# A decode step on one core: the score matmuls of a K chunk as a four-pass loop on TensorE

## The chip, the cores and the metric

The kernel runs on one core of one Trainium2 chip. The metric is device time in microseconds (us) for one execution, lower is better. Times are medians of several executions. A profile is one execution recorded by the hardware profiler; its span goes from the first to the last instruction on the core.

The engines named here are TensorE (PE; its weight loads are PEld), VectorE (DVE), ScalarE (ACT), GpSimd (POOL) and SyncE (SP). Each runs its own list of instructions in order and waits on semaphores that others raise. In this kernel SyncE issues the large transfers.

## The reference

One token passes through a transformer block: layer norm, grouped-query attention against a long cache, layer norm, a gated feed-forward layer, with residual sums. `x` is 1 x 1024; there are 32 query heads and 4 K/V heads of 128, the cache holds 65536 positions, the feed-forward layer is 3584 wide, everything in bf16.

```
q = (layernorm(x) @ wq) as 32 heads of 128
scores = q . k * 128**-0.5          # each K/V head serves 8 query heads
o = softmax(scores) . v             # over 65536 positions
h = x + o @ wo
h2 = h + (gelu(layernorm(h) @ w_gate) * (layernorm(h) @ w_up)) @ w_down
```

K and V together are 134 MB, the weights 39 MB: each byte is read once.

## The kernel before

**Layout.** A K/V head has 65536 positions, 512 on each of 128 partitions. A chunk is 64 of these 512, that is 128 x 64 positions of 128 numbers, 2 MB; a head has NCH = 8 chunks of K and 8 of V. One load brings two chunks of K (4 MB), or two or four chunks of V (4 or 8 MB), into `ring`, a buffer of NSL = 4 slots of 4 MB that every large transfer uses in turn (`load`, L238, and `chunk`, L76). A slot can be loaded again when whatever read it has finished.

**Scores of a chunk** (`k_chunk`, L251). VectorE takes the chunk in NS = 4 quarters (s) and transposes each in blocks of 32 x 32, as 4-byte pairs (L264), from the ring into a tile `kt`. So it is VectorE that frees a K slot, after eight such transposes (two chunks). For each quarter TensorE runs four matmuls (jt = 0 to 3, L268), whose weights are parts of `qs`, a copy of the head's queries spread with zeros (`make_qs`, GpSimd, L222 and L226). All 16 add into one PSUM bank `qk`. Afterwards (`score_chunk`, L272) VectorE transposes `qk` into `sc` (L278) and takes a maximum (L279). `sc` holds four chunks, so a head has two of them.

**Softmax of a head** (`softmax_head`, L281). Over the eight maxima VectorE and TensorE form one bias per query head (L284 to L294: maximum, transpose, maximum, diagonal, broadcast, scaling); then ScalarE computes 16 exponentials (L301) from the two `sc` tiles into two `pt` tiles, with row sums.

**V of a head** (`v_chunk`, L308). TensorE multiplies `pt` with V straight from the ring, 16 matmuls per chunk (L317), and so frees V slots. After the last chunk ScalarE copies the sum (L326), TensorE folds it in eight matmuls (L329), VectorE copies the outcome to `o_raw` (L331).

**Order.** The loop at L335 goes over the four heads g and their chunks ci: K chunk, then the scores of the chunk before, at the head's end the last scores and the softmax, and after chunks 3 and 7 four V chunks of the head before. The V of the last head comes after that, then the output projection and the feed-forward layer, whose weights go through the same ring. The code does not write out waits. The framework that builds the program records which tiles each instruction reads and writes, orders the instructions of each engine by priority and by its own estimate of when they are ready, and sets the semaphores. Within an engine the order is then fixed. What comes out for VectorE in a K load is: eight transposes L264, then L278, L279, L278, L279.

```
for g in range(Hkv):
    for ci in range(NCH):
        k_chunk(g, ci)
        if ci >= 1:
            score_chunk(g, ci - 1)
        if ci == NCH - 1:
            score_chunk(g, ci)
            softmax_head(g)
```

SyncE's order of loads is: two of wq, four of K of head 0, two of K of head 1, V of head 0 (4 MB and 4 MB), two of K of head 1, V of head 0 (8 MB), and from there on two loads of K and 8 MB of V in turn, with the last 16 MB of V, wo, w_gate, w_up and w_down behind them.

## Time and profile before

| what | value |
|---|---|
| median of 3 executions | 410.69 us (410.64 to 410.88) |
| profiled execution, span | 408.8 us |
| outside the span (median less span) | 1.9 us |
| moved by transfers | 173 MB, mean 424 GB/s |
| TensorE busy | 228.8 us, 56% |
| VectorE busy | 205.1 us, 50% |
| ScalarE busy | 36.6 us, 9% |
| GpSimd busy | 43.5 us, 11% |
| mean granted TensorE clock | 0.787 of full speed |

The profiled execution's own time is not listed beside the others; its span is the one in the table. In a timeline line the numbers are the start and the length in us, then engine, source line, operation, output and input, with the shape, and xN for N instructions merged; in brackets stand the idle time before it and what ended it. In a line of waits the numbers are the total in us, how many, and the longest. In a group's line they are, behind the bar, the busy time in us, the mean of one in ns, and the engine's idle time before them with what ended it. A matmul's duration includes its tail, which overlaps the next one: the rate is better read from the distance of weight loads, one of which goes with each matmul.

### The profile page before, as it was taken

To read this page: it belongs to the slowest core of one execution; us is meant where nothing else is said; L and a number is where in the kernel's file an instruction comes from. 1 tells how busy PE (TensorE), PEld (TensorE's weight loads), DVE (VectorE), ACT (ScalarE), POOL (GpSimd) and SP (SyncE) were. 2 spreads that over 40 slices of the span, in tenths; PEclk is the share of its full clock that TensorE was granted. 3 is DMA by queue.
4 is the path that set the end of the run, shared out by engine and by line. 5 is a ranking of instruction groups with operands and counts; after the bars stand their busy time and mean duration, and the time that the engine had idled before them with its cause. 6 is when DMAs were issued, how large, how long until landed. Compare 5 with 4: busy or idle time off the path is not lost.

```text
span 408.8 us, 3981 instructions
## 1 busy us (share of the span) xinstructions
PE 228.8 (56%) x1623; PEld 99.0 (24%) x1623; DVE 205.1 (50%) x263; ACT 36.6 (9%) x136; POOL 43.5 (11%) x150
## 2 busy tenths in 40 slices
PE   1337677688388367844765575576351425275045
PEld 1112222133133132311222222222120113143024
DVE  2118999999299239905980696089500001012010
ACT  1000000070000520000008000000340000000000
POOL 8123000300000400000002400000400100002000
PEclk9966989988888668868996689669885656566688
DMA  8999999999999999999999999999999999999995
GB/s 359 410 462 406 442 430 418 449 415 452 417 457 430 402 444 458 423 410 428 472 417 420 418 478 394 428 462 430 436 418 449 430 442 425 427 432 423 416 410 212
DMA packets 5144, 173.26 MB, mean 424 GB/s; under 512 B 643, under 2 KB 647, under 8 KB 1031
## 3 DMA queue, kind: packets, MB, share of 16 engines
q1 hardware_dynamic: 5079, 173.02, 98.4%
q8 instruction: 12, 0.20, 0.2%
q14 instruction: 5, 0.04, 0.0%
q10 hardware_dynamic: 48, 0.00, 0.0%
HBM read 173.02 MB, written 0.00 MB: 423 GB/s over the span
## 4 chain that ended last, share of the span: by engine, by line
DMA 68%; DVE 22%; PE 5%; issue 4%; SPq 0%; ACT 0%
DMA ring<-in_A_k_cache_dram 42%; DVE kt L264 19%; DMA ring<-in_A_wo_dram 8%; DMA ring<-in_B_w_up_dram 7%; DMA ring<-in_A_v_cache_dram 7%; DMA ring<-in_B_w_down_dram 4%; PE qk_ps L268 2%; PE at_ps L410 2%; PE acc_ps L317 1%; DVE sc L278 1%; DVE mx L279 1%; SPq L100 0%; PE mxT_ps L286 0%; PE d_ps L489 0%; DVE gm L288 0%
## 5 line engine op out<-in xcount | busy, mean ns | idle before, releaser
L268 PE MATMUL qk_ps<-kt,qs 128*128 128x512 bf16 x512 | 141.0, 426 | 59.8 <-DVE kt L264 46.2
L264 DVE STREAM_TRANSPOSE kt<-ring 128x1024 f32<-128x1024 f32 x128 | 146.2, 1208 | 45.4 <-DMA ring<-in_A_k_cache_dram 45.4
L268 PEld LDWEIGHTS <-qs 128*128 128x128 bf16 x512 | 53.7, 105 | 143.8 <-issue 95.1
L317 PE MATMUL acc_ps<-ring,pt 128*32 128x512 bf16 x512 | 44.7, 526 | 50.6 <-DMA ring<-in_A_v_cache_dram 50.6
L301 ACT ACTIVATE pt<-sc,nbias 128x256 bf16<-128x256 f32 x64 | 31.5, 494 | 261.9 <-DVE nbias L294 261.9
L317 PEld LDWEIGHTS <-pt 128*32 128x32 bf16 x512 | 18.4, 127 | 75.2 <-issue 51.8
L331 DVE COPY o_raw<-o_ps 128x8 f32<-128x8 f32 x4 | 0.7, 167 | 48.1 <-PE o_ps L329 48.1
L278 DVE STREAM_TRANSPOSE sc<-qk_ps 128x512 f32<-128x512 f32 x32 | 22.1, 692 | 1.0 <-PE qk_ps L268 1.0
L279 DVE TENSOR_REDUCE mx<-sc 128x8 f32<-128x512 f32 x32 | 22.0, 688 | 1.1
L222 POOL MEMSET qs<- 128x2048 bf16 x4 | 7.2, 1802 | 94.8 <-PE qk_ps L268 94.8
L186 PEld LDWEIGHTS <-xz 128*32 128x32 bf16 x192 | 6.8, 124 | 33.0 <-issue 16.1
L226 POOL COPY qs<-qsel 32x32 bf16<-32x32 bf16 x64 | 11.2, 247 | 16.6 <-DVE qsel L217 15.9
L324 DVE TENSOR_TENSOR lsum<-lpart 128x8 f32<-128x8 f32 x4 | 0.7, 164 | 24.2 <-ACT pt L301 24.2
L186 PE MATMUL qw_ps<-ring,xz 128*32 128x512 bf16 x64 | 7.2, 625 | 9.4 <-DMA ring<-in_A_wq_dram 9.4
L410 PE MATMUL at_ps<-ring,o2z 128*32 128x512 bf16 x64 | 6.6, 594 | 10.4 <-DMA ring<-in_A_wo_dram 10.4
L301 ACT ACTIVATION_READ_ACCUMULATOR pt<-sc,nbias 128x1 f32 x64 | 12.0, 187 | 0.0
L186 PE MATMUL u_ps_w<-ring,xz 128*32 128x512 bf16 (+1 forms) x64 | 4.5, 450 | 10.7 <-DMA ring<-in_B_w_up_dram 10.7
L427 DVE TENSOR_TENSOR h_col<-hc_ps,x_col 128x8 f32<-128x8 f32 x1 | 0.2, 166 | 19.5 <-PE hc_ps L420 19.5
L199 DVE STREAM_TRANSPOSE u_ps_r<-u_ps_w 128x512 f32<-128x512 f32 (+1 forms) x2 | 1.2, 629 | 14.1 <-PE u_ps_w L186 14.1
L199 DVE STREAM_TRANSPOSE q_r<-qw_ps 128x512 f32<-128x512 f32 x2 | 1.3, 696 | 13.6 <-PE qw_ps L186 13.6
L489 PE MATMUL d_ps<-ring,actz 128*32 128x128 bf16 x108 | 5.0, 263 | 5.6 <-DMA ring<-in_B_w_down_dram 5.5
L380 POOL MEMSET cz<- 128x256 bf16 x1 | 0.3, 311 | 72.6 <-PE qk_ps L268 72.6
(104 smaller groups left out, 92.0 us busy)
## 6 DMA issues: line engine op xcount, KB each, us to landing
ring<-in_A_k_cache_dram SPq DMA_DIRECT2D x16, 4096.0 KB
ring<-in_A_wq_dram SPq DMA_DIRECT2D x2, 4096.0 KB
ring<-in_A_v_cache_dram SPq DMA_DIRECT2D x2, 4096.0 KB
ring<-in_B_w_gate_dram SPq DMA_DIRECT2D x1, 7168.0 KB
ring<-in_B_w_up_dram SPq DMA_DIRECT2D x1, 7168.0 KB
ring<-in_B_w_down_dram SPq DMA_DIRECT2D x1, 4096.0 KB
ring<-in_B_w_down_dram SPq DMA_DIRECT2D x1, 1792.0 KB
ring<-in_B_w_down_dram SPq DMA_DIRECT2D x1, 768.0 KB
```

Of the source, the lines that this page charges most:

```text
L186: nc.tensor.matmul(banks[t // 4][32 * q:32 * q + 32, :], lhsT=rows_z[:, ci, :], rhs=w, start=first, stop=last, tile_position=(0, 32 * q))
L199: nc.vector.transpose(out=r[:, o:o + n].rearrange("p (e j) -> p e j", j=32) if sizes else r[:, o:o + n], in_=src)
L222: nc.gpsimd.memset(qs[:], 0.0)
L226: nc.gpsimd.tensor_copy(out=qs[rows, :, s, SQ * i + s:SQ * (i + 1):NS], in_=qsel[rows, :, g * rep:(g + 1) * rep])
L264: nc.vector.transpose(out=kt[:], in_=k32[:, s * W:(s + 1) * W])
L268: nc.tensor.matmul(qk[:], lhsT=st["qs"][:, jt, s, :], rhs=mv[:, :, J, :, t], start=(s == 0 and jt == 0), stop=(s == NS - 1 and jt == 3))
L278: nc.vector.transpose(out=sc.rearrange("p n h s -> p (n h s)"), in_=qk[:])
L279: nc.vector.tensor_reduce(out=st["mx"][:, :, ci], in_=sc.rearrange("p n h s -> p h n s"), axis=AX.XY, op=ALU.max)
L301: nc.scalar.activation(out=pt[:].rearrange("p c n h s -> p (c n) h s")[:, :, r, :], in_=sc[:].rearrange("p c n h s -> p (c n) h s")[:, :, ...
L317: nc.tensor.matmul(acc[32 * c:32 * c + 32, :], lhsT=pt[:, ci % CPH, n, :, :].rearrange("p h s -> p (h s)"), rhs=v_sb[:, n:CH:NN, :], start ...
L410: nc.tensor.matmul(at_ps[32 * q:32 * q + 32, :], lhsT=o2z[:, c, :], rhs=wv[:, c, :].rearrange("k (p s c) -> k s p c", s=DS, c=C4)[:, s], s ...
L489: nc.tensor.matmul((d_ps, d_odd)[q // 2][32 * q:32 * q + 32, :], lhsT=a_row[:, AZ - m:AZ - m + 32], rhs=w_row[:, j * OB:(j + 1) * OB], sta ...
```

## The change

The four quarters of a chunk are transposed into one `kt` tile of the whole chunk. Then VectorE sets the PSUM bank to zero, and TensorE runs its 16 matmuls as a loop of four passes (one per quarter) with four matmuls in each; the addresses in `qs` and `kt` come from a register. The loop stands in a critical section: the framework treats it as one unit, which TensorE enters when what was ordered before it is there, and the program is cut into blocks around it, so that each engine gets a jump at each cut. Since the loop's body is the same in every pass, the matmuls always add to what the bank holds. `kt` has 2 buffers of a chunk instead of 6 of a quarter, `sc` has 2 instead of 3. The scores of a chunk follow one chunk later also across heads, so the last scores and the softmax of a head come after the first K chunk of the next one.

```diff
-    ktpool = ctx.enter_context(tc.tile_pool(name="ktpool", bufs=6))
+    ktpool = ctx.enter_context(tc.tile_pool(name="ktpool", bufs=2))
...
-    scpool = ctx.enter_context(tc.tile_pool(name="scpool", bufs=3))
+    scpool = ctx.enter_context(tc.tile_pool(name="scpool", bufs=2))
...
         qk = ps_qk.tile([P, NN * SQ], F32, name="qk_ps", tag="qk")
+        kt = ktpool.tile([P, NS * W], F32, name="kt", tag="kt")
         for s in range(NS):
-            kt = ktpool.tile([P, W], F32, name="kt", tag="kt")
-            nc.vector.transpose(out=kt[:], in_=k32[:, s * W:(s + 1) * W])
-            mv = kt[:].bitcast(BF16).rearrange("p (n j b t) -> p n j b t", n=NN, j=2, t=2)
-            for jt in range(4):
-                J, t = divmod(jt, 2)
-                nc.tensor.matmul(qk[:], lhsT=st["qs"][:, jt, s, :], rhs=mv[:, :, J, :, t],
-                                 start=(s == 0 and jt == 0), stop=(s == NS - 1 and jt == 3))
+            nc.vector.transpose(out=kt[:, s * W:(s + 1) * W], in_=k32[:, s * W:(s + 1) * W])
+        mv = kt[:].bitcast(BF16).rearrange("p (s n j b t) -> p s n j b t", s=NS, n=NN, j=2, t=2)
+        nc.vector.memset(qk[:], 0.0)
+        with tc.tile_critical(no_gpsimd_drain=True):
+            with nc.tensor.Fori(0, NS) as i:
+                for jt in range(4):
+                    J, t = divmod(jt, 2)
+                    nc.tensor.matmul(qk[:], lhsT=st["qs"][:, jt, bass.ds(i, 1), :].rearrange("p s m -> p (s m)"),
+                                     rhs=mv[:, bass.ds(i, 1), :, J, :, t].rearrange("p s n b -> p (s n) b"),
+                                     start=False, stop=False, skip_group_check=True)
         st[("qk", ci)] = qk
...
+    def score_step(g, ci):
+        score_chunk(g, ci)
+        if ci == NCH - 1:
+            softmax_head(g)
+
+    late = None
     for g in range(Hkv):
         for ci in range(NCH):
             k_chunk(g, ci)
-            if ci >= 1:
-                score_chunk(g, ci - 1)
-            if ci == NCH - 1:
-                score_chunk(g, ci)
-                softmax_head(g)
+            if late:
+                score_step(*late)
+            late = g, ci
             if g >= 1 and ci % VB == VB - 1:
                 for vi in range(ci - VB + 1, ci + 1):
                     v_chunk(g - 1, vi)
+    score_step(*late)
```

## The prediction

> **What bounds the kernel now.** I read the page's totals first, then the DMA queue's own waits, then the timeline of each engine in the first head, then the groups by form.

> ```profile
> span 408.8 us, 3981 instructions
> PE 228.8 (56%) x1623; PEld 99.0 (24%) x1623; DVE 205.1 (50%) x263; ACT 36.6 (9%) x136; POOL 43.5 (11%) x150
> DMA  8999999999999999999999999999999999999995
> q1 hardware_dynamic: 5079, 173.02, 98.4%
> ```

> The transfers bound it: 173 MB, the queue 98.4% busy in every slice, engines half idle. A 4 MB load takes 9.7 us (K data reach VectorE at 150.16, 188.95, 228.12 and 266.90, four loads apart: 38.8/4). So the change costs nothing until it makes a load start late. A load starts when its ring slot is free, and K slots are freed by VectorE:

> ```profile
> SPq L247 <- DVE kt L264: 158.3, 15, 12.5
> SPq L247 <- PE acc_ps L317: 33.0, 6, 6.4
> ```

> How early a load is issued is the margin. In the first head VectorE sets the pace, with TensorE close behind it:

> ```profile
> 33.97 0.14 PEld L268 LDWEIGHTS <-qs 128*128 128x128 bf16 x1 [0.28 <-issue]
> 34.39 0.14 PEld L268 LDWEIGHTS <-qs 128*128 128x128 bf16 x1 [0.28 <-issue]
> 36.89 4.25 PEld L268 LDWEIGHTS <-qs 128*128 128x128 bf16 x20 [0.22 <-issue]
> 55.69 9.12 DVE L264 STREAM_TRANSPOSE kt<-ring 128x1024 f32<-128x1024 f32 x8
> 64.73 0.68 DVE L278 STREAM_TRANSPOSE sc<-qk_ps 128x512 f32<-128x512 f32 x1
> ...
> 67.39 9.12 DVE L264 STREAM_TRANSPOSE kt<-ring 128x1024 f32<-128x1024 f32 x8
> 89.39 12.10 SPq L247 DMA_DIRECT2D ring<-in_A_k_cache_dram  x2
> 102.31 3.64 PE L317 MATMUL acc_ps<-ring,pt 128*32 128x512 bf16 x64
> ```

> A pair of chunks (one load) takes VectorE 67.39-55.69 = 11.7 us: eight transposes 9.12, two score transposes, two maxima. The eighth K load is issued near 101.2 (89.39+12.10, less the 0.33 that an issue takes); the transfer ahead of it lands at 111.41 (where VectorE next waits for K data). The margin is 10 us over the five periods since the first pair: above 11.7+2.0 = 13.7 us per pair the transfers run dry.

> ```profile
> L264 DVE STREAM_TRANSPOSE kt<-ring 128x1024 f32<-128x1024 f32 x128 | 146.2, 1208 | 45.4 <-DMA ring<-in_A_k_cache_dram 45.4
> L278 DVE STREAM_TRANSPOSE sc<-qk_ps 128x512 f32<-128x512 f32 x32 | 22.1, 692 | 1.0 <-PE qk_ps L268 1.0
> L279 DVE TENSOR_REDUCE mx<-sc 128x8 f32<-128x512 f32 x32 | 22.0, 688 | 1.1
> L469 DVE MEMSET d_ps<- 128x128 f32 x1 | 0.2, 165 | 0.1
> L424 DVE MEMSET hc_ps<- 128x8 f32 x1 | 0.1, 65 | 0.0
> L301 ACT ACTIVATE pt<-sc,nbias 128x256 bf16<-128x256 f32 x64 | 31.5, 494 | 261.9 <-DVE nbias L294 261.9
> ```

> **The change, part by part.** In the changed program VectorE's order per pair is: eight K transposes, score transpose of each chunk, two maxima, two memsets. TensorE enters each loop behind a list of waits: all four transposes of its chunk and, because a critical section closes everything ordered before it, whatever stands earlier in the program: for the pair's first loop (A) also the first transpose of the second chunk, for its second (B) the score transpose of the first chunk; besides, loads already issued and exponentials already ordered. So A starts after five transposes, B after A and a score transpose, and VectorE's second score transpose waits for the end of B, with the next pair's transposes queued behind it. Before, matmuls ran four per transpose, beside them; now B runs beside nothing. The period is a sum:

> - Five transposes, 9.12/8 each: 5.70. The other three hide under loop A.
> - Loop A, 16 matmuls. TensorE has idled some 9 us (3.0+5.7) and starts slow: in the fence above weight loads come 427 ns apart after an idle stretch, ten of them, then 20 in 4.25 us, 212 ns. 10x0.4275+6x0.2125 = 5.55.
> - Loop control shows in no row. A pass: below, nothing, as the sequencer may run ahead of the array; above, a weight load plus one sequencer step as long as a DMA issue (0.10+0.33 = 0.43). I take one exposed weight load, 0.105 (L268, PEld), four per loop: 0.42, since a weight load is what a branch most directly delays. Entry: below 0.14 (a transpose ends at 33.44, the first matmul starts at 33.58), above 0.7 (SyncE's wait at the start barrier); taken 0.45. Exit: below 0.17 (the tail of a matmul, 378 against 212 ns apart), above 1.0; taken 0.55, since drain and two semaphore hops come in series. A: 6.97.
> - Score transpose 0.70, between A and B.
> - Loop B, at 0.2125 without a pause: 3.40+0.42+1.00 = 4.82.
> - Score transpose 0.70, two maxima 2x0.67, two new memsets. 65 ns at 8 columns, 165 at 128: 0.83 ns per column, 0.49 at 512. Sum 3.02.

> Period 21.2 us against 11.7, bounds 19.0 (no control cost beyond 0.17 exit and 0.14 entry) and 25.2 (upper ones). It passes 13.7, so the chain of pairs sets the time in head 0, and also later: a head moves eight loads, 77.6 us, 19.4 per pair.

> [...]

> Moved work. Softmax of a head now follows the next head's first transposes. In head 0 to 1, VectorE's order mixes these with scores, so they cover a loop: an estimated 4 us saved. In the other two boundaries VectorE stands in order behind the copy of the previous head's output, so TensorE's V block (3.64), its copy and fold (0.7+1.06+0.3), then maximum, diagonal and bias (1.8, from 290.55 to 292.35) come before the next transposes: 7.5 less the 3.0 that VectorE does meanwhile. The next loop also waits for 16 exponentials, 7.9 us against 5.7 of transposes. 4.4+2.2, twice: 13. The middle V block of a head hides beside scores and transposes. SyncE's queue keeps its order; its loads wait for slots. The V blocks stand behind the loops on TensorE and free V slots with them, later by the same periods. Waits on issued loads bind once: the first loop A needs the second K load, 9.9 after the first, against 5.7: 4.1. Later loads land over 4 us ahead of the loop that names them. Fewer buffers: kt holds two chunks where it held one and a half, so VectorE still runs a pair ahead at most; a third sc buffer is missed only when a head's first scores come before the first eight exponentials, 3.9 us, which the five transposes cover. Branches on the other engines lie in their idle time.

> Sum: first transpose 32.3, +4.1, fifteen periods 318.0, -4, +13, last eight transposes 9.1: K is done at 372.5. Then the V load that waits for it starts, 2.0 later (the last output transfer, 406.81 to the end), with an empty queue. Before, that V load could start at 295.9, when its predecessor landed (TensorE's V block waits until 295.97); from there the span had 112.9 us of transfers at full rate, which are unchanged. 372.5+2.0+112.9 = 487.4. Outside the span lie 410.7-408.8 = 1.9 us, the median less the span: **489 us**, 19% slower.

> **The rivals.**
> 1. Cheaper loops: period 19.0, 33 us less, 456. For: the sequencer may hide all control under slow matmuls. Against: below 19.4 the transfers bind in the later heads and keep part of it.
> 2. Dearer loops: a pass at 0.43 adds 8x0.33 = 2.6 per pair, 39 us: 528. For: each pass reads registers and branches; against: ten matmuls run slow and cover it.
> 3. TensorE stays slow through both loops (pauses at each pass keep it so): +1.29 and +3.44 per pair, 71 us: 560. Against: four matmuls per 1.14 us transpose, a quarter of it idle, stayed fast in the pair at 44 us.
> [...]
> 5. Not slower: transfers hide it all, 410.7. It needs a period under 13.7, hence A+B under 4.3 us; 32 matmuls at 212 ns are 6.8. Only if loops run beside the transposes, VectorE's own 12.9 setting the pace, would it hold; the listed waits speak against it.

> **How the numbers follow.** Forecast 0.55, rivals 0.12, 0.14, 0.09, 0.07, 0.03. 489 is the forecast's. The range leaves out 560 and 410.7 and the thin ends: 452 to 540. About 0.2% can be told from no change here. Faster 0.01, same 0.02, slower 0.97.

> **What to look for.** Pair starts of K transposes 21 us apart in every head, and not 38.8 per two; VectorE's second score transpose waiting about 5 us for TensorE; loop matmuls 427 then 212 ns apart; DMA share near 84%, with gaps in slices from the first head to the third; a full queue only after the last K transpose near 372. Wrong if matmuls of a chunk start before its fourth transpose, if loop B is far from 4.8 us, or if SyncE's K issues still come 10 us ahead of need.

## The result and the profile after

The changed kernel takes 493.12 us (median of 4 executions, 491.98 to 493.64) against 410.74 us: 1.2005 times as long, with an interval of 1.199 to 1.2019. The forecast was 489.0 with a range of 452 to 540. The profiled execution took 493.34 us, with a span of 491.6 and a mean granted clock of 0.785 (0.787 before), so the clock is not what moved.

The totals of the page after the change:

```profile
span 491.6 us, 5288 instructions
PE 232.5 (47%) x1623; PEld 99.4 (20%) x1623; DVE 218.1 (44%) x295; ACT 36.6 (7%) x136; POOL 43.6 (9%) x150
DMA  8999995727087999999589989958956999999994
q1 hardware_dynamic: 5079, 173.02, 83.5%
```

Read the rows beside those of before. No engine does much more work: TensorE 232.5 us against 228.8, VectorE 218.1 against 205.1 (32 memsets more). The same 173.02 MB pass through the queue, but it is 83.5% busy instead of 98.4%, and the row of slices, counted from 0, shows where: gaps from slice 6 to slice 30 (74 to 381 us), then a full queue nearly to the end. One slice (123 to 135 us) is empty. While K is read, the queue now runs dry again and again, though several slices between the gaps are still full: the transfers no longer set the pace there.

Who holds SyncE's loads back, from the waits of the DMA queue:

```profile
SPq L247 <- DVE kt L264: 271.9, 15, 29.4
SPq L247 <- PE acc_ps L321: 74.2, 6, 13.1
```

Before, the 15 K loads waited 158.3 us for VectorE to free a slot, now 271.9, and the longest wait has grown from 12.5 to 29.4 us. The V loads wait 74.2 instead of 33.0. So VectorE reads K late. Why it does stands in the groups and the waits:

```profile
L271 PE MATMUL qk_ps<-kt,qs 128*128 x512 | 156.8, 453 | 171.1 <-DVE kt L264 93.1
L264 DVE STREAM_TRANSPOSE kt<-ring 128x1024 f32<-128x1024 f32 x128 | 146.4, 1205 | 3.7 <-DMA ring<-in_A_k_cache_dram 3.7
L282 DVE STREAM_TRANSPOSE sc<-qk_ps 128x512 f32<-128x512 f32 x32 | 22.9, 716 | 136.5 <-PEq L267 136.4
L283 DVE TENSOR_REDUCE mx<-sc 128x8 f32<-128x512 f32 x32 | 19.9, 657 | 0.0
L266 DVE MEMSET qk_ps<- 128x512 f32 x32 | 15.5, 485 | 3.0 <-issue 0.2
```

The K transposes waited 45.4 us for data before and wait 3.7 now: data are always there. VectorE's idle time has moved to the score transpose, 136.4 us, released by TensorE's sequencer at L267, the critical section. TensorE in turn waits 93.1 us for the K transposes. Each waits for the other, once per pair of chunks.

One such pair in the timeline (the second of head 0; weight loads left out except in the pause that they show):

```profile
58.68 9.09 DVE L264 STREAM_TRANSPOSE kt<-ring 128x1024 f32<-128x1024 f32 x8
65.17 5.34 PE L271 MATMUL qk_ps<-kt,qs 128*128 x16 [9.58 <-DVE kt L264]
...
70.68 0.72 DVE L282 STREAM_TRANSPOSE sc<-qk_ps 128x512 f32<-128x512 f32 x1 [2.91 <-PEq L267]
...
72.15 4.39 PE L271 MATMUL qk_ps<-kt,qs 128*128 x16 [1.65 <-DVE sc L282]
73.29 0.58 PEld L271 LDWEIGHTS qk_ps<-kt,qs 128*128 x4 [0.50 <-issue]
...
76.72 0.72 DVE L282 STREAM_TRANSPOSE sc<-qk_ps 128x512 f32<-128x512 f32 x1 [5.33 <-PEq L267]
77.36 1.24 DVE L283 TENSOR_REDUCE mx<-sc 128x8 f32<-128x512 f32 x2
78.70 1.03 DVE L266 MEMSET qk_ps<- 128x512 f32 x2
79.64 3.46 DVE L264 STREAM_TRANSPOSE kt<-ring 128x1024 f32<-128x1024 f32 x3
```

From 58.68 to 79.64 is one period, 20.96 us, against 11.7 before. Loop A starts after the fifth transpose (which ends at 64.4), loop B after the first score transpose, and VectorE idles 5.33 us under loop B with the next pair's transposes behind it.

### The profile page after: what moved, and what is told of

The parts are those of the page before. It is cut to its first block, busy times and chain, and to the rows that moved or that the text cites. A ratio compares the mean times of both kernels' runs of the same rounds, so it can differ in the third digit from the quotient of the medians.

```text
span 491.6 us, 5288 instructions
## 1 busy us (share of the span) xinstructions
PE 232.5 (47%) x1623; PEld 99.4 (20%) x1623; DVE 218.1 (44%) x295; ACT 36.6 (7%) x136; POOL 43.6 (9%) x150
## 3 DMA queue, kind: packets, MB, share of 16 engines
q1 hardware_dynamic: 5079, 173.02, 83.5%
HBM read 173.02 MB, written 0.00 MB: 352 GB/s over the span
## 5 line engine op out<-in xcount | busy, mean ns | idle before, releaser
L271 PE MATMUL qk_ps<-kt,qs 128*128 x512 | 156.8, 453 | 171.1 <-DVE kt L264 93.1
L264 DVE STREAM_TRANSPOSE kt<-ring 128x1024 f32<-128x1024 f32 x128 | 146.4, 1205 | 3.7 <-DMA ring<-in_A_k_cache_dram 3.7
L271 PEld LDWEIGHTS qk_ps<-kt,qs 128*128 x512 | 56.5, 110 | 269.9 <-issue 245.8
L282 DVE STREAM_TRANSPOSE sc<-qk_ps 128x512 f32<-128x512 f32 x32 | 22.9, 716 | 136.5 <-PEq L267 136.4
L321 PE MATMUL acc_ps<-ring,pt 128*32 128x512 bf16 x512 | 32.3, 410 | 22.3 <-DMA ring<-in_A_v_cache_dram 14.4
L305 ACT ACTIVATE pt<-sc,nbias 128x256 bf16<-128x256 f32 x64 | 31.5, 494 | 140.6 <-DVE nbias L298 140.6
L321 PEld LDWEIGHTS <-pt 128*32 128x32 bf16 x512 | 15.5, 103 | 38.6 <-issue 29.2
L330 ACT COPY acc_sb<-acc_ps 128x512 f32<-128x512 f32 x4 | 2.3, 586 | 245.2 <-PE acc_ps L321 245.2
L283 DVE TENSOR_REDUCE mx<-sc 128x8 f32<-128x512 f32 x32 | 19.9, 657 | 0.0
L266 DVE MEMSET qk_ps<- 128x512 f32 x32 | 15.5, 485 | 3.0 <-issue 0.2
L226 POOL COPY qs<-qsel 32x32 bf16<-32x32 bf16 x64 | 11.2, 247 | 17.2 <-DVE qsel L217 16.5
L186 PE MATMUL g_ps_w<-ring,xz 128*32 128x512 bf16 (+1 forms) x64 | 5.2, 505 | 6.6 <-DMA ring<-in_B_w_gate_dram 6.6
```

The costliest lines, as they stand in the source:

```text
L186: nc.tensor.matmul(banks[t // 4][32 * q:32 * q + 32, :], lhsT=rows_z[:, ci, :], rhs=w, start=first, stop=last, tile_position=(0, 32 * q))
L226: nc.gpsimd.tensor_copy(out=qs[rows, :, s, SQ * i + s:SQ * (i + 1):NS], in_=qsel[rows, :, g * rep:(g + 1) * rep])
L264: nc.vector.transpose(out=kt[:, s * W:(s + 1) * W], in_=k32[:, s * W:(s + 1) * W])
L266: nc.vector.memset(qk[:], 0.0)
L271: nc.tensor.matmul(qk[:], lhsT=st["qs"][:, jt, bass.ds(i, 1), :].rearrange("p s m -> p (s m)"), rhs=mv[:, bass.ds(i, 1), :, J, :, t].rearr ...
L282: nc.vector.transpose(out=sc.rearrange("p n h s -> p (n h s)"), in_=qk[:])
```

## The experiments

The changes that the new kernel makes together were taken apart. Each kernel was timed against the kernel before on the same chip (410.60 to 410.72 us there).

**e1: the late order alone**, in the kernel before.

```diff
+    late = None
     for g in range(Hkv):
         for ci in range(NCH):
             k_chunk(g, ci)
-            if ci >= 1:
-                score_chunk(g, ci - 1)
-            if ci == NCH - 1:
-                score_chunk(g, ci)
-                softmax_head(g)
+            if late:
+                score_step(*late)
+            late = g, ci
...
+    score_step(*late)
```

> The kernel before with the late order alone: scores and softmax follow one chunk later across heads, matmuls unrolled as before, buffers as before. Theory (the wait chain of the critical loop costs the time): the pair of chunks keeps its 11.7 us on VectorE, so 410.7 us, within 0.5. Rival (the late scores and softmax cost it, through V blocks and exponentials that come later): each of three head boundaries adds 2 to 6 us as in the changed kernel, 415 to 425 us.

Measured: 410.70 us, ratio 1.0 (0.999 to 1.0009). The order of scores and softmax cost nothing by itself here.

**e2: the memset and the always-adding matmuls alone**, in the kernel before.

```diff
+        nc.vector.memset(qk[:], 0.0)
...
-                                 start=(s == 0 and jt == 0), stop=(s == NS - 1 and jt == 3))
+                                 start=False, stop=False, skip_group_check=True)
```

> The kernel before with the memset of the PSUM bank alone, and matmuls that always add. Theory: the pair takes VectorE 11.7 + 2 x 0.485 = 12.7 us, below the 13.7 at which the transfers run dry, so 410.7 us, within 0.5. Rival (VectorE's added work is on the path): 32 x 0.485 = 15.5 us more, 426 us.

Measured: 411.12 us, ratio 1.0014 (1.0005 to 1.0023), 0.4 us.

**e3: all of the change but the loop and its critical section.** The 16 matmuls are written out, one `kt` tile per chunk, two buffers, memset, two `sc` buffers, late order.

```diff
-        with tc.tile_critical(no_gpsimd_drain=True):
-            with nc.tensor.Fori(0, NS) as i:
-                for jt in range(4):
...
+        for s in range(NS):
+            for jt in range(4):
+                J, t = divmod(jt, 2)
+                nc.tensor.matmul(qk[:], lhsT=st["qs"][:, jt, s, :], rhs=mv[:, s, :, J, :, t],
+                                 start=False, stop=False, skip_group_check=True)
```

> The changed kernel with the loop and its critical section taken out: 16 matmuls written out with fixed addresses, one kt tile of a chunk with 2 buffers, memset, 2 sc buffers, late scores. Theory: matmuls start again after the first transpose or at the latest beside the next chunk's; VectorE sets the pace with 12.7 us per pair, 410.7 us, within 1. Rival (the one kt tile with 2 buffers and fewer sc buffers make the chain): a period near 19 to 21 us stays and with it more than 450 us.

Measured: 410.70 us, ratio 1.0003 (0.9993 to 1.0012). So the whole loss sits in the loop and the section around it; buffers, tile size, memset and order carry none of it that can be told at this noise.

**e4: the critical section kept, the loop written out inside it.**

```diff
         with tc.tile_critical(no_gpsimd_drain=True):
-            with nc.tensor.Fori(0, NS) as i:
+            for s in range(NS):
                 for jt in range(4):
```

> The changed kernel with the critical section kept, but its 16 matmuls written out instead of the loop of four passes: no registers, no branch per pass. Theory (the unit with its waits is the cost, the passes a small part): the pauses between passes of the second loop go, three of 0.28 us, and some 0.3 to 0.5 us of control; the period falls from 21.0 to about 19.6 us, 15 x 1.4 = 20 us less, 465 to 480 us. Rival (register addresses and branches are the cost): back to 411 us.

Measured: 480.67 us, ratio 1.1708 (1.1686 to 1.173), just above the theory's 480. The timeline of its second pair:

```profile
56.20 9.10 DVE L264 STREAM_TRANSPOSE kt<-ring 128x1024 f32<-128x1024 f32 x8
62.37 5.59 PE L271 MATMUL qk_ps<-kt,qs 128*128 128x512 bf16 x16 [9.26 <-DVE kt L264]
...
68.22 0.72 DVE L281 STREAM_TRANSPOSE sc<-qk_ps 128x512 f32<-128x512 f32 x1 [2.92 <-PEq L267]
69.37 3.66 PE L271 MATMUL qk_ps<-kt,qs 128*128 128x512 bf16 x16 [1.41 <-DVE sc L281]
73.20 0.72 DVE L281 STREAM_TRANSPOSE sc<-qk_ps 128x512 f32<-128x512 f32 x1 [4.26 <-PEq L267]
...
76.12 3.46 DVE L264 STREAM_TRANSPOSE kt<-ring 128x1024 f32<-128x1024 f32 x3
```

The shape of the changed kernel without any loop: a period of 19.9 us. What the loop adds can be read line by line. B takes 3.66 us here and 4.39 there; the first matmul of B follows the score transpose after 0.43 us here (68.94 to 69.37) and 0.75 there (71.40 to 72.15). Of the 82.4 us lost, 12.5 go with the loop and 69.9 remain with the section and its waits. The theory had put some 20 us on the loop, 1.4 per pair, and jumps and entries do save that much here; but loop A took longer without the loop, 5.85 us on average over the 16 pairs against 5.41. It started at other places of the grid on which the granted clock changed (last section): in pairs two to four the slow rate lasted 4.1 to 5.0 us here and 2.9 to 3.4 there.

**e6: two passes of eight matmuls** in place of four of four.

```diff
-            with nc.tensor.Fori(0, NS) as i:
-                for jt in range(4):
+            with nc.tensor.Fori(0, NS // 2) as i:
+                for h in range(2):
+                    for jt in range(4):
...
```

> The changed kernel with two passes of eight matmuls instead of four of four. Theory: the pause between passes shows only where matmuls run fast (0.28 us in the second loop of a pair, hidden under 427 ns matmuls in the first); two pauses fewer in the second loop and up to one in the first, 0.6 to 0.8 us per pair, 9 to 12 us less: 481 to 484 us. Rival (passes are the main cost): half of the 82 us goes, 452 us.

Measured: 486.96 us, ratio 1.1869 (1.1835 to 1.1902). That is 3 us above the theory's 481 to 484; the rival's 452 was far off. The 6.2 us gained are half of the loop's 12.5, but this does not price a pass: the one jump that is left hardly shows (loop B takes 3.7 to 3.8 us in most pairs, against 3.66 written out and 4.3 to 4.4 with four passes). What the loop still costs beside e4 lies mainly in its entry, which stays at 0.75 to 1.05 us where e4 has 0.43 to 0.66.

**e5: the score transposes moved off the chain.** Scores follow two chunks late, and on VectorE each score transpose is ordered behind the K transposes of the chunk two later, so that loops can run beside transposes.

```diff
...
-        nc.vector.transpose(out=sc.rearrange("p n h s -> p (n h s)"), in_=qk[:])
+        tr = nc.vector.transpose(out=sc.rearrange("p n h s -> p (n h s)"), in_=qk[:])
+        tc.add_manual_dep(tr.ins, last_t[0].ins.name,
+                          mybir.DependencyInfo(mybir.DependencyClass.NoSync, mybir.DependencyReason.DATA), reason="order")
...
-            if late:
-                score_step(*late)
-            late = g, ci
+            late.append((g, ci))
+            if len(late) > 2:
+                score_step(*late.pop(0))
...
```

> The changed kernel with loop and critical section, but scores two chunks late, and each score transpose put in VectorE's order behind the transposes of the chunk two later, so that it finds its loop done. Theory in its simplest form (VectorE's wait for the loop just started, with the next transposes queued behind it, is the whole cost): the period falls to VectorE's own 12.9 us or TensorE's two loops with entries, 12 to 13.5 us, and the time to 411 to 425 us. Rival (the critical section's other waits, for loads issued earlier in the order, hold the loops as soon as the chain is shorter): VectorE's transposes wait on kt buffers held by loops that wait for loads, and the time stays at 450 to 475 us.

Measured: 475.17 us, ratio 1.1572 (1.1552 to 1.1591). The simple theory fell. Behind the first pair of head 0 the pairs do come 12.1 to 13.7 us apart (transposes at 49.35, 63.06, 76.22, 88.32), about as it said. So the jumps at the section's block cuts, which every engine still makes here, can't cost much by themselves: they fit into 12.1 to 13.7 us beside everything else. In head 1 the timeline shows something else:

```profile
131.20 0.33 SPq L247 DMA_DIRECT2D ring<-in_A_v_cache_dram  x1
...
133.19 31.69 SPq L247 DMA_DIRECT2D ring<-in_A_k_cache_dram  x2
...
153.86 5.28 PE L273 MATMUL qk_ps<-kt,qs 128*128 x16 [16.65 <-DMA ring<-in_A_v_cache_dram]
159.31 1.25 DVE L266 STREAM_TRANSPOSE kt<-ring 128x1024 f32<-128x1024 f32 x1 [16.70 <-PEq L269]
```

A score loop, which reads no V, waits 16.65 us for an 8 MB load of V, because that load stands before the section in the program. VectorE's transposes queue up behind it for 16.70 us, the K slot stays occupied, and of the two K loads in the third line the second is issued only at 164.5 us (133.19 + 31.69, less the 0.33 of an issue). The load that the loop waits for was issued at 131.20, 1.7 us before the loop ahead of it started; while it moves only one more is issued, and from 154 to 165 us the queue is 66% busy. The second theory, that the section's other waits take over, holds; its range of 450 to 475 was passed by 0.2 us.

**e9: the same order, the loop written out in the section.** Is it the loop's length or the section's list of waits that keeps e5 slow?

```diff
         with tc.tile_critical(no_gpsimd_drain=True):
-            with nc.tensor.Fori(0, NS) as i:
+            for s in range(NS):
                 for jt in range(4):
```

> e5's order (scores two chunks late, score transposes behind later K transposes on VectorE) with the critical section kept but its 16 matmuls written out, no loop. Theory (from head 1 on the waits on issued loads in the critical section bind, whatever the loop costs): 466 to 476 us, at most 9 below e5's 475.2. Rival (the loop's control and entry made e5's matmuls too slow to hide): 411 to 445 us.

Measured: 470.89 us, ratio 1.1451 (1.1423 to 1.148), inside the theory's bounds. The same stall stands at the same place of its timeline:

```profile
151.54 6.40 PE L273 MATMUL qk_ps<-kt,qs 128*128 128x512 bf16 x16 [17.90 <-DMA ring<-in_A_v_cache_dram]
158.11 1.25 DVE L266 STREAM_TRANSPOSE kt<-ring 128x1024 f32<-128x1024 f32 x1 [19.08 <-PEq L269]
```

It is not the only one: by the list of TensorE's waits in this run, score matmuls wait five times for a load of V, 70.8 us in all, the longest 17.9. So the section keeps the kernel slow in either of two ways: through the chain of score transposes when VectorE's order is as the framework writes it, and through waits on loads that it does not read when the chain is shortened. A register-addressed loop outside such a section was not tried.

**e8: no section, but whole chunks.** Does the mere fact hurt that a loop starts with the fourth transpose of its chunk, not with the first? In e3 the quarters were taken in an order that makes the first matmul need the last quarter.

```diff
-        for s in range(NS):
+        for s in (3, 0, 1, 2):
             for jt in range(4):
```

> The written-out matmuls of e3 (no loop, no critical section), but with the chunk's fourth quarter first, so that the first of the 16 matmuls needs the chunk's fourth transpose, as the loop does. Theory (the critical section's list of waits is what costs, not the loss of quarter-by-quarter work by itself): the fourth transpose ends 4.6 us into the pair, 16 slow matmuls' worth of about 5.6 follow, then the second chunk's 3.4, and the second score transpose, two maxima and two memsets end near 15 us: a period of 14 to 15.5 in head 0, against a threshold of 13.7, hidden again later: 411 to 418 us. Rival (starting only when the whole chunk is transposed is most of the loss): periods near 20, 460 or more.

Measured: 410.71 us, ratio 1.0007 (0.9994 to 1.002): no change, where the theory had 411 to 418. Its second and third pairs:

```profile
44.98 4.59 DVE L264 STREAM_TRANSPOSE kt<-ring 128x1024 f32<-128x1024 f32 x4
49.50 0.68 DVE L280 STREAM_TRANSPOSE sc<-qk_ps 128x512 f32<-128x512 f32 x1
...
49.63 10.04 PE L270 MATMUL qk_ps<-kt,qs 128*128 128x512 bf16 x32 [3.13 <-DVE kt L264]
...
56.23 0.72 DVE L280 STREAM_TRANSPOSE sc<-qk_ps 128x512 f32<-128x512 f32 x1 [0.95 <-PE qk_ps L270]
...
58.57 4.59 DVE L264 STREAM_TRANSPOSE kt<-ring 128x1024 f32<-128x1024 f32 x4
```

Without a section the framework may put a chunk's score transpose behind the next four K transposes, and TensorE runs 32 matmuls in one block with VectorE beside it. The pairs come 13.6 and then 12.5 us apart, below or at the prediction's bound of 13.7. Waiting for the whole chunk cost nothing here.

**e7: TensorE kept busy ahead of loop A.** Ten extra matmuls, whose output is not read, run during the first transposes of each pair.

```diff
+        if ci % 2 == 0:
+            warm = misc([P, NN * SQ], F32, "warm")
+            for _ in range(10):
+                nc.tensor.matmul(warm[:], lhsT=st["qs"][:, 0, 0, :], rhs=mv[:, 0, :, 0, :, 0], start=True, stop=True)
```

> The changed kernel with ten extra matmuls, whose output nobody reads, on TensorE during the transposes of the first chunk of each pair, so that its first loop starts fast. Theory: the first loop then takes what the second does, 4.36 instead of 5.1 to 5.3 us, as pauses between passes come into view; 0.8 to 0.9 us per pair, 12 to 14 us less: 479 to 481 us. Rival (the slow start costs its full 10 x 0.215 = 2.1 us per pair): 32 us less, 461 us. If the extra matmuls only delay the loop: no change or slower.

Measured: 469.63 us, ratio 1.1426 (1.1399 to 1.1453): 23.5 us below the changed kernel, between theory and rival, which were both 9 us or more off. Loop A takes 4.31 us in the second pair instead of 5.34. But it runs that fast (4.3 to 4.4 us) in only 8 of the 16 pairs and takes 5.1 to 6.6 in the others, and this is not where most of the gain lies. By the starts of the pairs, the first four pairs together gain 2.3 us (the fifth starts at 118.07 instead of 120.36). The two pairs of the first head boundary gain 4.5 (35.81 instead of 40.32), the three around the second 6.5 (176.21 to 238.70 instead of 181.93 to 250.94), the three around the third 9.1 (259.64 to 320.46 instead of 273.10 to 343.03): 20.1 of the 21.8 us by which the last pair is ahead. The extra matmuls also changed what VectorE does at the boundaries. How much of these gains is the clock and how much the order stays open.

## Why the prediction was right, point by point

**The bound: right; the threshold: only bracketed.** The transfers hide a longer period up to a point: e8's first four periods, 12.8 us on average with one of 13.6, stay hidden, the changed kernel's 21 does not. No run that kept its pairs between 13 and 19 us through a whole kernel was made, so the 13.7 itself was not tested. The queue ran empty where it was predicted, between head 0 and the last K transpose, at 83.5% ("near 84%").

**The period: right in the sum, with errors that cancel.** The eight undisturbed pairs average 21.09 us (20.06 to 22.16), forecast 21.2. So near a hit is luck: in the pair shown loop A with entry and exit took 0.66 us less than forecast, loop B 0.50 more. By terms:

| term | forecast, us | measured, us |
|---|---|---|
| five transposes | 5.70 | 5.7 |
| A: entry | 0.45 | 0.8 |
| A: matmuls and passes | 5.97 | 5.34, its tail included |
| A: exit | 0.55, tail included | 0.17 |
| score transpose | 0.70 | 0.72 |
| B: entry, matmuls and passes, exit | 4.82 | 5.32 (0.75 + 4.39 + 0.18) |
| score transpose, maxima, memsets | 3.02 | 2.92 |

The mis-sized terms are the loop's control. The forecast spread it evenly (0.42 for the passes of each loop). It is not even: in the loop A shown the slow matmuls cover the passes completely (0.427 us apart across them), in loop B each of the three jumps shows: the matmuls on its two sides start 0.42 to 0.51 us apart in the pair shown where 0.22 is usual, so a jump costs 0.20 to 0.29. Entry costs 0.75 to 0.8 in head 0 and 0.86 to 1.05 later, not 0.45, and exit only the 0.17 that was its lower bound: in the pair shown TensorE's drain at L267 ends at 70.53 us, with the last matmul (70.51), and VectorE's transpose starts at 70.68. e4, which has a section but no jumps, confirms the attribution: B 3.66 without a pause, its entry 0.43.

**Ten slow matmuls: misread, and a fixed count was the wrong rule.** The stretch that the ten were read from has eight, from 33.59 to 36.89 us, 3.3 us:

```profile
33.59 0.10 PEld L268 LDWEIGHTS <-qs 128*128 128x128 bf16 x1 [2.85 <-issue]
33.97 0.14 PEld L268 LDWEIGHTS <-qs 128*128 128x128 bf16 x1 [0.28 <-issue]
...
36.53 0.14 PEld L268 LDWEIGHTS <-qs 128*128 128x128 bf16 x1 [0.28 <-issue]
36.89 4.25 PEld L268 LDWEIGHTS <-qs 128*128 128x128 bf16 x20 [0.22 <-issue]
```

With eight in place of ten, 2 x 0.215 us less in each of fifteen periods, the forecast would have been by estimate 6.5 us lower, near 482.5. The same profile also has a stretch of 13 (229.41 to 234.86 us), which shows that no one count holds. After the change, from the first weight load of loop A to the change of rate, the eight undisturbed pairs took 2.9 to 3.8 us in six cases and 5.8 in two, 3.8 on average; the forecast had 4.3 in each. What sets it stands in the last section.

**Head boundaries: close.** Against two ordinary pairs each, the boundary 0 to 1 cost -1.9 us (forecast -4); the other two together 12.6 (forecast 13). The cause is the one named. The timeline at the boundary 1 to 2, where the bias of the last head is done just ahead of the transposes and the loop then waits for its exponentials:

```profile
206.66 0.17 DVE L298 TENSOR_SCALAR nbias<-bc_ps 128x8 f32<-128x8 f32 x1 [0.48 <-PE bc_ps L296]
206.74 9.12 DVE L264 STREAM_TRANSPOSE kt<-ring 128x1024 f32<-128x1024 f32 x8
215.47 5.28 PE L271 MATMUL qk_ps<-kt,qs 128*128 x16 [8.85 <-ACT pt L305]
```

The first pair cost 5.3 more than an ordinary one (forecast 4.1).

**The end of K and the tail.** K was done at 373.80 (forecast 372.5), so all period errors together came to 1.3 us. The tail took 117.8 us instead of 114.9: the windows after 373.8 us move 47.3 MB (374 GB/s in 11.2 us, 477 in 15, 420 in 40, 423 in 35, 261 in 16.6), those of before after 296.0 us 45.8 MB (422 in 14, 431 in 40, 424 in 40, 304 in 18.8). The term took the time at which one load landed for the time at which the next one began; 1.5 MB more were left, by estimate some 3.5 us at 424 GB/s; the tail was 2.9 us longer than forecast. With the 1.3 us of K these 2.9 are the whole difference of the profiled span, 491.6 against 487.4.

**The rivals.** Cheaper loops (456) fell: even with no loop at all e4 takes 480.67. Dearer passes (528) fell: 0.2 to 0.3 us each, in one loop of two. A slow clock in both loops (560) fell: loop B's matmuls start 0.22 us apart within a pass in all pairs but the two of the first head boundary. A long stall at every jump (523, chance 0.07) fell: the 96 jumps back in the loops took TensorE's sequencer 0.21 to 0.23 us each, and the instruction queue moved the same 12 packets as before:

```profile
q8 instruction: 12, 0.20, 0.2%
```

No pass in the loop A shown has a pause, and those of loop B have 0.2 to 0.3 us. The last rival, not slower, was given a condition that turned out not to suffice: "only if loops run beside the transposes". e5 brought that about in head 0 and still took 475.17 us. The prediction said that waits on issued loads bind once; that holds for the changed kernel, where everything runs late enough for the loads to be there, and would not hold for a faster one (16.65 us in e5).

## What to carry to other kernels

A critical section is priced by what its entry waits for, not by what it contains: here some 70 of 82 us came from closing over everything ordered before it, and only 12.5 from the loop itself. Before a loop is put into a kernel whose engines overlap by fine-grained waits, list what the section will wait for, find the other engine's next instruction that waits for its end, and add up that chain per period against the slack that transfers leave. Loads that stand before the section in the program are on that list, even if the section doesn't read them (16.65 us for one such load in e5).

## What the runs showed of the hardware

```profile
65.14 0.56 PEld L271 LDWEIGHTS qk_ps<-kt,qs 128*128 x3 [9.99 <-issue]
...
68.11 0.14 PEld L271 LDWEIGHTS qk_ps<-kt,qs 128*128 x1 [0.28 <-issue]
68.54 1.47 PEld L271 LDWEIGHTS qk_ps<-kt,qs 128*128 x7 [0.28 <-issue]
```

The prediction counted ten slow matmuls in one stretch; in these loops what held was the place of the start on the grid, not a count.

**Which jumps showed.** In loop A matmuls 0.427 us apart stayed 0.427 apart across a pass. In loop B, at 0.22 us, those on the two sides of a jump start 0.45 us apart in the median of all pairs. The rate at the jump is not all that counts: the last row above holds the seven weight loads behind the change to the full rate, the third jump among them, and that one shows no pause either (0.22 us). The trace also has a record of every branch on TensorE's sequencer. The 96 jumps back took 0.21 to 0.23 us each, in loops A and B alike. But in the loop A above the branch that ends the last pass starts at 69.06 us, 1.07 us before the loop's last matmul (70.13); in the fifteen loops A that start slow this lead is 0.72 to 2.18 us. In loop B of the same pair it is 0.05 us (76.12 and 76.17), and at most 0.09 in the fourteen loops B that run at the full rate throughout. So in these loops the jumps showed where this lead was under 0.1 us, and at the slow rate, where it was 0.72 us or more at the end, they were covered. The weight loads say the same: in the slow part of loop A one starts 0.43 us before its matmul (68.11 and 68.54), in loop B the first one of a pass just 0.03 us before (73.29 and 73.32).
